# Moving an output weight to the end of a cached-attention kernel, and peeling and halving its last block

## The chip, the cores and the metric

One core of a Trainium2 chip. The metric is the device time of one execution in microseconds (us). The span of a trace is some 2 us shorter than the time of the same execution: the profiled execution of the kernel before took 2552.9 us and its trace spans 2551.1. Where two kernels are compared in time, it is by runs on the same chip; where single steps are compared, it is by the traces.

## The reference, cut to what matters

```python
def _A_ref(x, k_cache, v_cache, wq, wo):          # H = 16 heads, Dh = 256, 65536 keys
    q = (x @ wq).reshape(B, Sq, H, Dh)...          # one query row
    scores = einsum("bhqd,bhkd->bhqk", q, k_cache) * (Dh ** -0.5)
    p = softmax(scores)
    o = einsum("bhqk,bhkd->bhqd", p, v_cache)
    return o.reshape(B, Sq, H * Dh) @ wo           # wo: 4096 x 448

xn = layernorm(x)
s = _A_ref(xn, k_cache, v_cache, wq, wo)
g = silu(silu(xn @ w1) @ w2)
return x + s * g
```

All is bf16. The K and V caches are 537 MB each, and everything else is small.

## The kernel before

The keys are worked through in 64 blocks, four to a head. A block is two K loads and two V loads of 4 MB. VectorE multiplies 19 of every 32 columns of K by the query itself and hands 13 over to ScalarE as products. When a block's scores are there, TensorE and VectorE find one maximum over all partitions ("rows", "gmax", "bcast"), ScalarE takes the exponentials, and TensorE sums them with V ("attend": 64 matmuls of 512 columns) and transposes the result ("turn"). A block's V is loaded and attended while the next block's K is scored.

Two words on TensorE's clock: the profile shows the clock that it was granted as a share of full speed. "Warm" means 1.00, and 32 V matmuls then took 7.07 us; "cold" means 0.50. In a timeline, the bracket at the end of a line gives the time for which the engine had been idle and what ended it.

```python
    def sp_block(i):                                 # the order of the loads
        for t in range(TPB):                         # TPB = 2
            take(sp, kf[t])                          # K buffer t is free
            sp.dma_start(out=Kt[t][:, :], in_=src(Kd, i, t)).then_inc(kl[t], 16)
            take(sp, vf[t])                          # V buffer t is free
            sp.dma_start(out=Vt[t][:, :], in_=src(Vd, i - 1, t)).then_inc(vl[t], 16)
    ...
        need("sp", t8)                               # at the start, once q is computed from W
        sp.dma_start(out=W[:, 0 : NHA * D]..., in_=A_wo...).then_inc(dl["wo"], 16)
    ...
        with nc.Fori(1, NBLK, 1, ...) as i:          # NBLK = 64
            sp_block(i)
            dve_block(i)
            act_block(i)
            act_keep(i - 1)
            pe_bcast()
            pe_attend()
            pe_rows()
            pe_turn()

        last = NBLK - 1                              # V of the last block, and the end
        for t in range(TPB):
            take(sp, vf[t])                          # vf[1] comes with the turn of the block before
            sp.dma_start(out=Vt[t][:, :], in_=src(Vd, last, t)).then_inc(vl[t], 16)
            take(sp, kf[t])
        dve_gmax(); pe_bcast(); act_softmax(last, own)
        ...                                          # the gate g (its reciprocal takes 2.94 us)
        pe_attend(); pe_turn(); act_keep(last)
        ...                                          # weights of 64 blocks, sums, 32 wo matmuls, output
```

## Time and profile before

| | before |
|---|---|
| time, median of 3 runs | 2550.97 us |
| bytes loaded | 1084.3 MB |
| rate of the body | 432 GB/s |
| span of the trace | 2551.1 us |
| last load landed | 2524.9 us |
| TensorE, VectorE, ScalarE busy | 50%, 87%, 57% |

A profile like this is read from the loads inward. The loads fill the body, so only the places where the queue is empty or slow are worth looking at: here the first 64 us and the last 40. The prediction below shows the lines.

### The profile page before, as it was taken

Reading aid. Unit: us, or ns where it says so; the run is one execution under the profiler, and the core shown is the slowest. Engines: PE = TensorE matmul, PEld = TensorE weight load, DVE = VectorE, ACT = ScalarE, POOL = GpSimd, SP = SyncE. Lnnn points to the kernel's source line nnn. Section 1 sums busy time; section 2 is a strip of 40 time slices with the busy share of each in tenths; the row PEclk is TensorE's granted clock in tenths of the full one; section 3 lists DMA queues with packets and bytes.
Section 4 is the critical chain, followed back from the end, with each engine's and each line's share of the span. In section 5 each row is a group of like instructions: output and inputs, shape, how many; then the busy total and the mean of one; then the engine's idle time right before and its main releaser. Section 6 shows DMA issues by size and latency. Waiting matters only on the chain. (4 is left out here: it accounts for less than half of the span.)

```text
span 2551.1 us, 30406 instructions
## 1 busy us (share of the span) xinstructions
PE 1285.1 (50%) x4876; PEld 478.1 (19%) x4876; DVE 2218.4 (87%) x10264; ACT 1445.4 (57%) x6990; POOL 1.2 (0%) x11
## 2 busy tenths in 40 slices
PE   3445545544554554455445445545544554455456
PEld 1111111211211111111112112111111121121122
DVE  5898898888988988988988889889889889898894
ACT  4555565555656555555655556565555555565552
POOL 0000000000000000000000000000000000000000
PEclk7777777777777777777777767777776677677768
DMA  9999999999999999999999999999999999999994
GB/s 386 432 430 434 430 434 430 433 431 432 431 432 432 432 432 431 432 432 432 432 431 432 431 433 431 433 433 432 432 432 431 432 431 432 431 432 432 431 432 210
DMA packets 39535, 1084.43 MB, mean 425 GB/s; under 512 B 4194, under 2 KB 6244, under 8 KB 6308
## 3 DMA queue, kind: packets, MB, share of 16 engines
q1 hardware_dynamic: 39522, 1084.31, 99.0%
q8 instruction: 3, 0.05, 0.0%
q14 instruction: 8, 0.07, 0.0%
q10 hardware_dynamic: 2, 0.00, 0.0%
HBM read 1084.29 MB, written 0.00 MB: 425 GB/s over the span
## 5 line engine op out<-in xcount | busy, mean ns | idle before, releaser
L241 ACT ACTIVATE junk_a<-prod 128x256 bf16<-128x256 bf16 x3328 | 1330.7, 401 | 754.2 <-ACTq L136 754.2
L288 PE MATMUL psO<-V,PV 128*2 128x512 bf16 x4096 | 1170.4, 456 | 1114.0 <-PEq L136 1114.0
L206 DVE CUSTOM_DVE_ANT_0 junk_d<-K,qcur 128x256 bf16<-128x256 bf16 x4864 | 1699.0, 415 | 0.0
L288 PEld LDWEIGHTS psO<-V,PV 128*2 128x2 bf16 x4096 | 388.6, 96 | 1869.4 <-issue 1536.8
L192 DVE TENSOR_TENSOR prod<-K,qcur 128x3328 bf16<-128x3328 bf16 x256 | 483.1, 1887 | 258.7 <-DVEq L136 258.7
L241 ACT ACTIVATION_READ_ACCUMULATOR junk_a<-prod 128x1 f32 x3328 | 619.8, 186 | 0.0
L206 DVE DVE_READ_ACCUMULATOR2_ANT S<- 128x1 f32 x4864 | 380.6, 78 | 0.0
L272 ACT COPY O<-psO 2x512 f32<-2x512 f32 x64 | 36.7, 574 | 222.5 <-ACTq L136 222.5
L309 PE MATMUL ps_t<-eye,O 2*128 2x1 f32 x512 | 68.4, 251 | 50.0 <-PEq L136 50.0
L309 PEld LDWEIGHTS ps_t<-eye,O 2*128 2x128 f32 x512 | 64.9, 191 | 70.5 <-issue 70.5
L274 ACT COPY hist<-ps_t 128x2 f32 x64 | 10.2, 160 | 89.9 <-ACTq L136 89.9
L278 PE MATMUL ps_nb<-gmax,ones_row 1*128 1x1 bf16 x64 | 10.1, 158 | 56.2 <-PEq L136 55.6
L182 DVE COPY qcur<-qb 128x256 bf16 (+1 forms) x64 | 14.6, 227 | 27.4 <-issue 16.1
L261 ACT ACTIVATE PV<-S,hist 128x128 bf16<-128x128 f32 x64 | 25.7, 402 | 2.1
L223 DVE COPY S<-S 128x128 f32<-128x128 f32 x64 | 14.5, 227 | 9.3
L299 PE MATMUL ps_m<-ident,rmax 128*1 128x128 bf16 x64 | 14.1, 220 | 9.3 <-PEq L136 9.3
L171 DVE TENSOR_REDUCE gmax<-ps_m 1x1 bf16<-1x128 f32 x64 | 17.5, 274 | 1.1 <-DVEq L136 1.1
L224 DVE TENSOR_REDUCE rmax<-S 128x1 bf16<-128x128 f32 x64 | 18.0, 281 | 0.0
L278 PEld LDWEIGHTS ps_nb<-gmax,ones_row 1*128 1x128 bf16 x64 | 6.0, 94 | 60.0 <-issue 59.7
L518 DVE TENSOR_REDUCE negM<-hist 128x16 f32<-128x64 f32 x1 | 0.3, 265 | 17.5 <-ACT hist L274 17.5
L441 PE MATMUL ps_a<-xnT,V 128*128 128x1 bf16 (+1 forms) x56 | 6.0, 208 | 15.6 <-DMA V<-in_B_w_dram 15.6
L261 ACT ACTIVATION_READ_ACCUMULATOR PV<-S,hist x64 | 11.9, 186 | 0.0
(56 smaller groups left out, 75.4 us busy)
## 6 DMA issues: line engine op xcount, KB each, us to landing
K<-in_A_k_cache_dram SPq DMA_DIRECT2D x128, 4096.0 KB, 21.5
V<-in_A_v_cache_dram SPq DMA_DIRECT2D x128, 4096.0 KB, 28.7
W<-in_A_wo_dram SPq DMA_DIRECT2D x1, 3584.0 KB, 25.2
W<-in_A_wq_dram SPq DMA_DIRECT2D x1, 3072.0 KB, 10.7
V<-in_B_w_dram SPq DMA_DIRECT2D x1, 1568.0 KB, 38.8
V<-in_B_w_dram SPq DMA_DIRECT2D x1, 1344.0 KB, 34.0
W<-in_A_wq_dram SPq DMA_DIRECT2D x1, 512.0 KB, 13.1
V<-in_B_w_dram SPq DMA_DIRECT2D x1, 224.0 KB, 35.0
```

The costliest lines, as they stand in the source:

```text
L171: dve.reduce_max(out=gmax[0:1, :], in_=ps_m[0:1, :], axis=AX.X).then_inc(gm, 1)
L182: q_t = own(dve.tensor_copy(out=qcur[:, :], in_=qb[:, sub(q0, Dh)]))
L192: m = dve.tensor_tensor(out=prod[k % 2][:, :, :], in0=Kv[:, s * SUB + ND : (s + 1) * SUB, :], in1=qcur[:, None, :].to_broadcast([P, NA, Dh ...
L206: ins = dve.tensor_tensor_reduce(out=junk_d[jk][:, :], in0=Kv[:, s * SUB + j, :], in1=qcur[:, :], scale=1.0, scalar=0.0, op0=ALU.mult, op1 ...
L223: dve.tensor_copy(out=S2[:, :], in_=S[:, :]).then_inc(kf[1], 1)
L224: dve.reduce_max(out=rmax[:, :], in_=S[:, :], axis=AX.X).then_inc(rm, 1)
L241: ins = act.activation(out=junk_a[jk][:, :], in_=prod[k % 2][:, j, :], func=ACT.Identity, accum_out=S[:, a : a + 1],)
L261: act.activation(out=PV[:, :], in_=S2[:, :], func=ACT.Exp, bias=neg, scale=scale, accum_out=hist[:, at(i), 1:2].rearrange("p o s -> p (o s)"),
L272: act.copy(out=O[:, :], in_=psO[:, :]).then_inc(oc, 1)
L278: pe.matmul(ps_nb[:, 0:1], lhsT=ones_row[0:1, :], rhs=gmax[0:1, :], start=True, stop=True).then_inc(bm, 1)
L288: ins = pe.matmul(psO[:, :], lhsT=PV[:, t * KT + 2 * c : t * KT + 2 * c + 2], rhs=Vt[t][:, c * 2 * Dh : (c + 1) * 2 * Dh], start=(t == 0 a ...
L309: ins = pe.matmul(ps_t[:, a : a + 1], lhsT=Ov[:, j, a, :], rhs=eye2[:, j : j + 1], start=(j == 0), stop=(j == 1),)
```

## The change

The intent is to have no load behind which nothing can start, and no work behind the last load that could have been done under it. `wo` is loaded last, in five pieces by heads, into the first K buffer. The last block is taken out of the loop and split in two halves, each with its own maximum and its own entry in the list of partial results, and the second half of its V goes into the weight buffer W, so that it waits for no turn. The weights of the first 15 heads and the gate are worked out under the last attends, and 30 of the 32 wo matmuls need nothing of the last head, so they run while its result is copied, turned and weighted. The core of the diff, with cuts:

```diff
-        need("sp", t8)
-        sp.dma_start(out=W[:, 0 : NHA * D]..., in_=A_wo...).then_inc(dl["wo"], 16)
 ...
         with nc.Fori(
-            1, NBLK, 1,
+            1, NBLK - 1, 1,
 ...
+        take(sp, kf[0]);  K(last, 0) -> Kt[0]
+        take(sp, vf[0]);  V(last - 1, 0) -> Vt[0]
+        take(sp, kf[1]);  halves(Kt[1], src(Kd, last, 1), (kl[1], kh))
+        take(sp, vf[1]);  V(last - 1, 1) -> Vt[1]
+        take(sp, vf[0]);  halves(Vt[0], src(Vd, last, 0), vh[0:2])
+        need("sp", t_wq)
+        halves(W, src(Vd, last, 1), vh[2:4])
+        take(sp, kf[0])
+        for (h0, h1), w in zip(pieces, wl):     # heads 0-4, 4-8, 8-12, 12-14, 14-16
+            sp.dma_start(out=wo_t[:, h0:h1, :], in_=wo_d[:, h0:h1, :]).then_inc(w, 16)
+
+        dve_block(last, halves=True)
+        act_block(last, halves=True)
+        pe_bcast()
+        pe_attend(between=half_max)             # block 62; first half's maximum in between
+        half_max(); dve_gmax(); act_keep(last - 1); pe_turn()
+        act_softmax(last + 1, own, KT, TPB * KT)
+        ... sums, weights and outputs of heads 0 to 14; the gate ...
+        ... 32 V matmuls (first half), 16 V matmuls, turn, 16 V matmuls ...
+        ... 8 wo matmuls, turn, 24 wo matmuls (the last head's weights beside them) ...
```

(Some lines are abridged to what they do; K(i, t) and V(i, t) stand for the load of half t of block i.)

More of the change, by code (lines that the diff above doesn't have):

```diff
@@ L46 @@
     NBLK = H * NB
+    NENT = NBLK + 1
+    H1 = H - 1
+    N1 = H1 * NB
+    NL = NENT - N1
     NA = SUB - ND
@@ L77 @@
     O = pool.tile([2, 2 * Dh], fp32, name="O")
-    hist = pool.tile([P, NBLK, 4], fp32, name="hist")
+    hist = pool.tile([P, NENT, 4], fp32, name="hist")
     ident = pool.tile([P, P], bf16, name="ident")
@@ L95 @@
     negM = pool.tile([P, H], fp32, name="negM")
-    cf = pool.tile([P, H, NB], fp32, name="cf")
-    wgt = pool.tile([P, H, NB], fp32, name="wgt")
+    cf = pool.tile([P, NENT], fp32, name="cf")
+    wgt = pool.tile([P, NENT], fp32, name="wgt")
     tot = pool.tile([P, H], fp32, name="tot")
-    part = pool.tile([P, H, 2, NB], fp32, name="part")
-    OT32 = pool.tile([P, H, 2], fp32, name="OT32")
-    OT = pool.tile([P, NHA], bf16, name="OT")
+    part = pool.tile([P, 2, NENT], fp32, name="part")
+    OT32 = pool.tile([P, 2, H], fp32, name="OT32")
+    OT = pool.tile([P, 2, H], bf16, name="OT")
     tmp = pool.tile([1, D], fp32, name="tmp")
@@ L105 @@
     psO = ps.tile([2, 2 * Dh], fp32, name="psO")
-    ps_m = ps.tile([1, P], fp32, name="ps_m")
+    ps_m = ps.tile([P, P], fp32, name="ps_m")
     ps_nb = ps.tile([P, 1], fp32, name="ps_nb")
@@ L111 @@
     ps_ao = ps.tile([1, D], fp32, name="ps_ao")
-    ps_tot = ps.tile([P, NBLK], fp32, name="ps_tot")
+    ps_tot = ps.tile([P, N1], fp32, name="ps_tot")
     eng = {"pe": pe, "dve": dve, "act": act, "gp": gp, "sp": sp}
@@ L146 @@
     sd, sa = sem("sd"), sem("sa")
-    dl = {n: sem(f"dl_{n}") for n in ("x", "wq", "w12", "wo", "out")}
+    dl = {n: sem(f"dl_{n}") for n in ("x", "wq", "w12", "out")}
+    kh = sem("kh")
+    vh = [sem(f"vh{t}") for t in range(4)]
+    pieces = ((0, 4), (4, 8), (8, 12), (12, 14), (14, 16))
+    wl = [sem(f"wl{t}") for t in range(len(pieces))]
     Kd = A_k_cache[0].rearrange("h (t p c) d -> (h t) p (c d)", p=P, c=KT)
@@ L171, in dve_gmax, with dve_block @@
         dve.reduce_max(out=gmax[0:1, :], in_=ps_m[0:1, :], axis=AX.X).then_inc(gm, 1)
-    def dve_block(i, first=False):
+    def dve_block(i, first=False, halves=False):
         n = [0]
@@ L183, in dve_block, with end @@
         used = [q_t] * 4
+        def end(c0, c1, f):
+            take(dve, pf, 2)
+            take(dve, sd, n[0])
+            n[0], used[:] = 0, [0] * 4
+            dve.tensor_copy(out=S2[:, c0:c1], in_=S[:, c0:c1]).then_inc(f, 1)
+            dve.reduce_max(out=rmax[:, :], in_=S[:, c0:c1], axis=AX.X).then_inc(rm, 1)
         for t in range(TPB):
@@ L189, in dve_block @@
                     take(dve, kl[t], 16)
-                if k >= 2:
+                if halves and k == 3:
+                    take(dve, kh, 16)
+                if k >= 2 and not halves:
                     take(dve, pf)
@@ L200, in dve_block @@
                 m.then_inc(mr, 1)
-                if k == 0 and not first:
+                if (k == 0 and not first) or (k == 2 and halves):
                     dve_gmax()
                 for j in range(ND):
-                    last = t == 0 and s == 1 and j == ND - 1
+                    last = t == 0 and s == 1 and j == ND - 1 and not halves
                     jk = 2 + t if last else j % 2
@@ L215, in dve_block @@
                     )
-                    ins.wait_op(sd, used[jk], "sem-ge")
+                    if used[jk]:
+                        ins.wait_op(sd, used[jk], "sem-ge")
                     if last:
@@ L220, in dve_block, with act_block @@
                         used[jk] = own(ins)
-        take(dve, pf, 2)
-        take(dve, sd, n[0])
-        dve.tensor_copy(out=S2[:, :], in_=S[:, :]).then_inc(kf[1], 1)
-        dve.reduce_max(out=rmax[:, :], in_=S[:, :], axis=AX.X).then_inc(rm, 1)
-    def act_block(i, first=False):
+            if halves:
+                end(t * KT, (t + 1) * KT, kf[t])
+        if not halves:
+            end(0, TPB * KT, kf[1])
+    def act_block(i, first=False, halves=False):
         n = [0]
@@ L254, in act_block, with act_softmax @@
                 act_softmax(i - 1, own)
+            if k == 2 and halves:
+                act_softmax(i, own, 0, KT)
         take(act, sa, n[0])
-    def act_softmax(i, own):
+    def act_softmax(i, own, c0=0, c1=TPB * KT):
         take(act, bm)
@@ L261, in act_softmax @@
         act.activation(
-            out=PV[:, :],
-            in_=S2[:, :],
+            out=PV[:, c0:c1],
+            in_=S2[:, c0:c1],
             func=ACT.Exp,
@@ L268, in act_softmax, with act_keep @@
         ).wait_op(sa, c, "sem-ge").then_inc(pv, 1)
-    def act_keep(i):
+    def act_keep(i, po=psO):
         take(act, od)
-        act.copy(out=O[:, :], in_=psO[:, :]).then_inc(oc, 1)
+        act.copy(out=O[:, :], in_=po[:, :]).then_inc(oc, 1)
         take(act, ho)
@@ L280, in pe_bcast, with pe_keys, pe_attend @@
         ).then_inc(bm, 1)
-    def pe_attend():
+    def pe_keys(po, T, k0, c0, n, start, stop, done=None):
+        for c in range(0, n, 2):
+            ins = pe.matmul(
+                po[:, :],
+                lhsT=PV[:, c0 + c : c0 + c + 2],
+                rhs=T[:, (k0 + c) * Dh : (k0 + c + 2) * Dh],
+                start=(start and c == 0),
+                stop=(stop and c == n - 2),
+            )
+        if done is not None:
+            ins.then_inc(done, 1)
+    def pe_attend(between=None):
         take(pe, pv)
-        n = KT // 2
         for t in range(TPB):
             take(pe, vl[t], 16)
-            for c in range(n):
-                ins = pe.matmul(
-                    psO[:, :],
-                    lhsT=PV[:, t * KT + 2 * c : t * KT + 2 * c + 2],
-                    rhs=Vt[t][:, c * 2 * Dh : (c + 1) * 2 * Dh],
-                    start=(t == 0 and c == 0),
-                    stop=(t == TPB - 1 and c == n - 1),
-                )
-            ins.then_inc(vf[0] if t == 0 else od, 1)
+            pe_keys(psO, Vt[t], 0, t * KT, KT, t == 0, t == TPB - 1, vf[0] if t == 0 else od)
+            if t == 0 and between:
+                between()
     def pe_rows():
@@ L417 @@
         t_q = t9
-        wo_n = W[:, 0 : NHA * D].rearrange("p (n d) -> p n d", d=D)
-        need("sp", t8)
-        sp.dma_start(
-            out=W[:, 0 : NHA * D].rearrange("p (h e) -> p h e", h=H),
-            in_=A_wo.rearrange("(h p a) d -> p h (a d)", p=P, a=2),
-        ).then_inc(dl["wo"], 16)
+        t_wq = t8
         need("dve", t_q0)
@@ L484, with halves @@
         last = NBLK - 1
-        for t in range(TPB):
-            take(sp, vf[t])
-            sp.dma_start(out=Vt[t][:, :], in_=src(Vd, last, t)).then_inc(vl[t], 16)
-            take(sp, kf[t])
-        dve_gmax()
-        pe_bcast()
+        hw = KT * Dh // 2
+        wo_t = Kt[0][:, 0 : NHA * D].rearrange("p (h e) -> p h e", h=H)
+        wo_n = Kt[0][:, 0 : NHA * D].rearrange("p (n d) -> p n d", d=D)
+        wo_d = A_wo.rearrange("(h p a) d -> p h (a d)", p=P, a=2)
+        def halves(T, s, sems):
+            for j in range(2):
+                w = slice(j * hw, (j + 1) * hw)
+                sp.dma_start(out=T[:, w], in_=s[:, w]).then_inc(sems[j], 16)
+        take(sp, kf[0])
+        sp.dma_start(out=Kt[0][:, :], in_=src(Kd, last, 0)).then_inc(kl[0], 16)
+        take(sp, vf[0])
+        sp.dma_start(out=Vt[0][:, :], in_=src(Vd, last - 1, 0)).then_inc(vl[0], 16)
+        take(sp, kf[1])
+        halves(Kt[1], src(Kd, last, 1), (kl[1], kh))
+        take(sp, vf[1])
+        sp.dma_start(out=Vt[1][:, :], in_=src(Vd, last - 1, 1)).then_inc(vl[1], 16)
+        take(sp, vf[0])
+        halves(Vt[0], src(Vd, last, 0), vh[0:2])
+        need("sp", t_wq)
+        halves(W, src(Vd, last, 1), vh[2:4])
+        take(sp, kf[0])
+        for (h0, h1), w in zip(pieces, wl):
+            sp.dma_start(out=wo_t[:, h0:h1, :], in_=wo_d[:, h0:h1, :]).then_inc(w, 16)
+        dve_block(last, halves=True)
+        act_block(last, halves=True)
         n = [0]
@@ L496, in own, with half_max, weights, v @@
             return n[0]
-        act_softmax(last, own)
+        def half_max():
+            pe_rows()
+            pe_bcast()
+        pe_bcast()
+        pe_attend(between=half_max)
+        half_max()
+        dve_gmax()
+        act_keep(last - 1)
+        pe_turn()
+        act_softmax(last + 1, own, KT, TPB * KT)
+        def weights(e0, e1, h0, h1, neg, p_tot):
+            n = e1 - e0
+            b = n // (h1 - h0)
+            def v(T):
+                return T.rearrange("p (h b) -> p h b", b=b)
+            def spread(T):
+                return T[:, h0:h1, None].to_broadcast([P, h1 - h0, b])
+            t = mark("dve", dve.tensor_reduce(
+                out=negM[:, h0:h1], in_=v(neg), axis=AX.X, op=ALU.min
+            ))
+            need("dve", t)
+            t = mark("dve", dve.tensor_tensor(
+                out=v(wgt[:, e0:e1]), in0=spread(negM), in1=v(neg), op=ALU.subtract
+            ))
+            need("act", t)
+            t = mark("act", act.activation(out=wgt[:, e0:e1], in_=wgt[:, e0:e1], func=ACT.Exp))
+            need("dve", t, p_tot[1])
+            t = mark("dve", dve.tensor_tensor(
+                out=cf[:, e0:e1], in0=wgt[:, e0:e1], in1=p_tot[0], op=ALU.mult
+            ))
+            need("dve", t)
+            t = mark("dve", dve.tensor_reduce(
+                out=tot[:, h0:h1], in_=v(cf[:, e0:e1]), axis=AX.X, op=ALU.add
+            ))
+            need("dve", t)
+            t = mark("dve", dve.reciprocal(out=tot[:, h0:h1], in_=tot[:, h0:h1]))
+            need("dve", t)
+            t = mark("dve", dve.tensor_tensor(
+                out=v(cf[:, e0:e1]), in0=v(wgt[:, e0:e1]), in1=spread(tot), op=ALU.mult
+            ))
+            need("dve", t)
@@ new lines, in outputs @@
+        def outputs(e0, e1, h0, h1):
+            b = (e1 - e0) // (h1 - h0)
+            t = mark("dve", dve.tensor_tensor(
+                out=part[:, :, e0:e1],
+                in0=hist[:, e0:e1, 2:4].rearrange("p e a -> p a e"),
+                in1=cf[:, None, e0:e1].to_broadcast([P, 2, e1 - e0]),
+                op=ALU.mult,
+            ))
+            need("dve", t)
+            t = mark("dve", dve.tensor_reduce(
+                out=OT32[:, :, h0:h1],
+                in_=part[:, :, e0:e1].rearrange("p a (h b) -> p a h b", b=b),
+                axis=AX.X,
+                op=ALU.add,
+            ))
+            need("dve", t)
+            return mark("dve", dve.tensor_copy(out=OT[:, :, h0:h1], in_=OT32[:, :, h0:h1]))
@@ L499 @@
+        tt = mark("pe", pe.matmul(
+            ps_tot[:, :], lhsT=ones_sq[:, :], rhs=hist[:, 0:N1, 1], start=True, stop=True
+        ))
+        weights(0, N1, 0, H1, hist[:, 0:N1, 0], (ps_tot[:, :], tt))
+        t_o = outputs(0, N1, 0, H1)
         t = mark("act", act.activation(out=g_e[0:1, :], in_=ps_y, func=ACT.Exp, scale=-1.0))
@@ L509 @@
         ))
-        pe_attend()
+        psO2 = ps_a[0:2, :]
+        take(pe, pv)
+        for j in range(2):
+            pe.wait_ge(vh[j], 16)
+            pe_keys(psO, Vt[0], j * KT // 2, j * KT // 2, KT // 2, j == 0, j == 1,
+                    od if j == 1 else None)
+        take(pe, pv)
+        t15 = mark("pe", pe.matmul(
+            ps_m[:, 0:NL], lhsT=ones_sq[:, :], rhs=hist[:, N1:NENT, 1], start=True, stop=True
+        ))
+        weights(N1, NENT, H1, H, hist[:, N1:NENT, 0], (ps_m[:, 0:NL], t15))
@@ L511 @@
+        act_keep(last)
+        pe.wait_ge(vh[2], 16)
+        pe_keys(psO2, W, 0, KT, KT // 2, True, False)
         pe_turn()
-        t_k = mark("act", act_keep(last))
+        pe.wait_ge(vh[3], 16)
+        pe_keys(psO2, W, KT // 2, KT + KT // 2, KT // 2, False, True, od)
+        t_k = mark("act", act_keep(last + 1, psO2))
         need("dve", t_k)
-        hv = hist[:, :, :].rearrange("p (h b) s -> p h b s", h=H)
-        neg = hv[:, :, :, 0]
-        t = mark("dve", dve.tensor_reduce(out=negM[:, :], in_=neg, axis=AX.X, op=ALU.min))
@@ L519 @@
-        need("dve", t)
-        t = mark("dve", dve.tensor_tensor(
-            out=wgt[:, :, :],
-            in0=negM[:, :, None].to_broadcast([P, H, NB]),
-            in1=neg,
-            op=ALU.subtract,
-        ))
-        need("act", t)
-        t = mark("act", act.activation(out=wgt[:, :, :], in_=wgt[:, :, :], func=ACT.Exp))
-        need("pe", t_k)
-        tt = mark("pe", pe.matmul(
-            ps_tot[:, :], lhsT=ones_sq[:, :], rhs=hist[:, :, 1], start=True, stop=True
-        ))
-        need("dve", t, tt)
@@ L533 @@
-        t = mark("dve", dve.tensor_tensor(
-            out=cf[:, :, :],
-            in0=wgt[:, :, :],
-            in1=ps_tot[:, :].rearrange("p (h b) -> p h b", h=H),
-            op=ALU.mult,
-        ))
-        need("dve", t)
-        t = mark("dve", dve.tensor_reduce(out=tot[:, :], in_=cf[:, :, :], axis=AX.X, op=ALU.add))
-        need("dve", t)
-        t = mark("dve", dve.reciprocal(out=tot[:, :], in_=tot[:, :]))
-        need("dve", t)
-        t = mark("dve", dve.tensor_tensor(
-            out=cf[:, :, :],
-            in0=wgt[:, :, :],
-            in1=tot[:, :, None].to_broadcast([P, H, NB]),
-            op=ALU.mult,
-        ))
@@ L550 @@
-        need("dve", t)
-        for a in range(2):
-            t = mark("dve", dve.tensor_tensor(
-                out=part[:, :, a, :], in0=hv[:, :, :, 2 + a], in1=cf[:, :, :], op=ALU.mult
-            ))
-        need("dve", t)
-        t = mark("dve", dve.tensor_reduce(
-            out=OT32[:, :, :], in_=part[:, :, :, :], axis=AX.X, op=ALU.add
-        ))
-        need("dve", t)
-        t = mark("dve", dve.tensor_copy(
-            out=OT[:, :], in_=OT32[:, :, :].rearrange("p h a -> p (h a)")
-        ))
@@ L565 @@
-        need("pe", t)
-        pe.wait_ge(dl["wo"], 16)
-        for n in range(NHA):
-            ins = pe.matmul(
-                ps_ao[0:1, :],
-                lhsT=OT[:, n : n + 1],
-                rhs=wo_n[:, n, :],
-                start=(n == 0),
-                stop=(n == NHA - 1),
-            )
+        t_l = outputs(N1, NENT, H1, H)
+        need("pe", t_o)
+        for (h0, h1), w in zip(pieces, wl):
+            pe.wait_ge(w, 16)
+            if h0 == pieces[1][0]:
+                pe_turn()
+            for h in range(h0, h1):
+                if h == H1:
+                    need("pe", t_l)
+                for a in range(2):
+                    ins = pe.matmul(
+                        ps_ao[0:1, :],
+                        lhsT=OT[:, a, h : h + 1],
+                        rhs=wo_n[:, 2 * h + a, :],
+                        start=(h == 0 and a == 0),
+                        stop=(h == H1 and a == 1),
+                    )
```

## The prediction

> **What bounds the kernel now.** I read the 40 slices of the page first, then the busy times by stretch, the DMA issues, and last the timeline of the final 60 us. The rows of the slices (DMA share in tenths, then GB/s moved) are
>
> ```profile
> DMA  9999999999999999999999999999999999999994
> GB/s 386 432 430 434 430 434 430 433 431 432 431 432 432 432 432 431 432 432 432 432 431 432 431 433 431 433 433 432 432 432 431 432 431 432 431 432 432 431 432 210
> ```
>
> The transfers fill every slice but the last. So the body can't be shortened by rearranging engines: 1084.3 MB at 432 GB/s are 2510 us. Only the first 64 us and the last 40 us are open. The busy times by stretch (us, busy time and count of each engine, granted clock, DMA share, GB/s) show them:
>
> ```profile
> 32.00:42.00 10.00, 0.00 (x0) 0.00 (x0) 10.00 (x44) 6.69 (x34) 0.00 (x0) 0.50 0.97 350
> 42.00:50.00 8.00, 5.96 (x56) 5.50 (x56) 8.00 (x40) 5.31 (x26) 0.00 (x0) 0.50 1.06 382
> 64.00:2500.00 2436.00, 1225.63 (x4621) 453.93 (x4621) 2162.26 (x10031) 1408.46 (x6839) 0.00 (x0) 0.72 1.00 432
> 2509.00:2512.00 3.00, 2.22 (x13) 0.88 (x10) 1.23 (x7) 0.57 (x1) 0.00 (x0) 1.00 0.05 22
> 2512.00:2525.00 13.00, 8.03 (x42) 3.52 (x42) 3.93 (x3) 1.25 (x5) 0.00 (x0) 1.00 0.80 323
> 2525.00:2551.00 26.00, 18.56 (x74) 7.29 (x74) 3.58 (x12) 0.99 (x3) 0.00 (x0) 0.78 0.00 1
> ```
>
> The queue stands empty from 2509 to 2512, and from 2525 on nothing is loaded while 26 us of closing work run. The timeline of the end (start, length, engine, line, operation) names that work:
>
> ```profile
> 2492.82 19.82 SPq L487 DMA_DIRECT2D V<-in_A_v_cache_dram  x2
> 2502.29 8.70 PE L288 MATMUL psO<-V,PV 128*2 128x512 bf16 x32 [9.57 <-PEq L136]
> 2511.82 1.07 PE L309 MATMUL ps_t<-eye,O 2*128 2x1 f32 x8 [0.78 <-PEq L136]
> 2514.32 7.07 PE L288 MATMUL psO<-V,PV 128*2 128x512 bf16 x32 [1.40 <-PEq L136]
> 2524.96 8.75 PE L288 MATMUL psO<-V,PV 128*2 128x512 bf16 x32 [3.57 <-PEq L136]
> 2535.93 0.27 DVE L518 TENSOR_REDUCE negM<-hist 128x16 f32<-128x64 f32 x1 [17.45 <-ACT hist L274]
> 2538.91 8.30 PE L568 MATMUL ps_ao<-W,OT 128*1 128x448 bf16 x32 [2.47 <-DVE OT L560]
> 2547.24 0.61 DVE L577 TENSOR_TENSOR tmp<-ps_ao,g_f 1x448 f32<-1x448 f32 x1 [8.39 <-PE ps_ao L568]
> 2548.53 0.32 SPq L585 DMA_DIRECT2D out_dram<-out_bf  x1
> ```
>
> The second last V load is issued only when TensorE has turned the block before (2512.3, hence the empty queue). It lands at 2524.9, and then all is serial: 8.75 us of V matmuls, 5.2 us of copies, turn and weights, 8.3 us of wo matmuls, 1.3 us of VectorE, 2.6 us for the output. At the start, wo is loaded where everything behind it waits (start us, length, issue; then the landing time of wo as 25.2 us):
>
> ```profile
> 27.62 0.38 SPq L422 DMA_DIRECT2D W<-in_A_wo_dram  x1
> 41.24 1.70 SPq L165 DMA_DIRECT2D K<-in_A_k_cache_dram  x1
> 62.64 1.89 DVE L192 TENSOR_TENSOR prod<-K,qcur 128x3328 bf16<-128x3328 bf16 x1 [2.85 <-DVEq L136]
> W<-in_A_wo_dram SPq DMA_DIRECT2D x1, 3584.0 KB, 25.2
> ```
>
> wo lands at 52.8. The first MLP weights ahead of it let TensorE start at 43.2, so wo has the queue for 9.6 us (3.67 MB at the 382 GB/s of that stretch), and block 1 starts only at 62.6, when its K has come in behind wo.
>
> **What the Trainium skill says.** "TensorE: Matmul & The Clock Gate", section "The HAM clock gate": the array runs at half clock after an idle window of about 3.4 us and at full clock after about that much activity. The trace agrees: 32 V matmuls took 7.07 us after a pause of 1.40 us, but 8.75 us after one of 3.57 us (clock 0.52 in its first stretch). "DMA: Bandwidth & Descriptors", section "Where 436 GB/s comes from": 435 GB/s at the SBUF ports, but about 358 from HBM per core. The trace has 432, so only the first binds here. "Runtime: NRT & Kernel Launch", section "Instruction fetch mechanics": code is fetched ahead in sequence, and a taken branch may stall. In the trace the loop's turn costs VectorE 16.1 us in 64 starts of a block, 0.25 each; the straight first block shows no hole. So I charge nothing for straight-line code in the peeled block.
>
> **The change part by part.**
> 1. wo leaves the start. K of block 1 is issued at 41.24 anyway (VectorE frees the buffer then), so it streams behind the MLP weights and lands 9.6 us earlier. Against it: queues that are ahead of the slowest run dry before 41.2, up to about 1.5 us. I take 9.3 us of shift for all of the body.
> 2. The last loads. V of block 62, second half, lands at 2502.2 - 9.3 = 2492.9. Behind it come 8.4 MB of V of block 63 without a hole, because the second half goes into W and waits for no turn. At the loop's own rate, 38.9 us for four loads, they take 19.4 us: landed at 2512.3. wo's 3.67 MB in five pieces take again 9.6 us: landed at 2521.9. The hole at 2509 is gone, the bytes are the same.
> 3. VectorE in the peeled block. Its first half ends at 2490.2 - 9.3 = 2480.9. Then come a copy and maximum (0.5), 1.9 + 6.6 us for 13 columns together and 19 single ones, 0.9 for waiting on and taking the first maximum, 8.5 for the last quarter, and 0.5 for the copy and maximum: 2499.8. TensorE asks for it only at 2501.6, so this is hidden by about 2 us.
> 4. TensorE's chain, which I take as the end-setter. Starting at 2492.9: V of block 62 second half, from a cold clock as before, 8.7 (2501.6). Maximum, row, broadcast 1.4 (2503.0). Turn with waits 1.2 (2504.2). Sums of the 15 heads 0.6 (2504.8). V of block 63 first half: 32 at the warm 7.07 (2511.9). Sum of five entries 0.2 (2512.1). 16 V matmuls 3.6 (2515.7; data there at 2507.6). Turn 1.2 (2516.9). 16 more 3.6 (2520.5; data there at 2512.3). wo of four heads, 8 matmuls at the warm 0.187 (20 of them took 3.8 us after 2543), 1.5 (2522.0). Turn 1.1 (2523.1). 24 more wo matmuls 4.5 (2527.6). VectorE 1.3, output 2.6: **2531.5**.
> 5. What disappears from the path: the weights and sums of 15 heads (about 3 us), the silu gate with its 2.94 us reciprocal, most of one cold start, and some of the wo matmuls' cold part. The last head's weights (about 0.7 us of VectorE after the last turn) lie beside the 24 wo matmuls.
> So of some 30 us of idle queue about 19.5 go. The closing matmuls (32 V, 32 V, 32 wo, some 20 us warm) are not removed, and TensorE falls behind the loads.
>
> **The rivals.**
> (a) The loads set the end. The last wo piece lands at 2521.9; four matmuls, VectorE and the output add 4.7: 2527. For it: wo is the last thing loaded. Against it: TensorE can't have begun the last two heads before 2526.9, 5 us later.
> (b) wo at the start was nearly free, because block 1 could not have begun earlier. Then there is no shift: about 2541. Against it is VectorE's wait of 2.85 us before 62.64 on K, and a body that is full to the last.
> (c) The clock falls back to half in the run of small matmuls at 2501 to 2505. Then 16 or so V matmuls cost twice: 3.5 us more, 2535. Before, the same small work between 2511 and 2514 left the clock at 1.00, so I give this one chance in five. The peeled code stalling on fetch, or VectorE's halves overrunning their 2 us, would add 1 to 4 us in the same way.
> (d) Slower than before: loading wo last puts 9.6 us behind the last V, which would cost if nothing left the start and the wo matmuls ran after the last piece alone. That makes about 2550.
>
> **Range and chances.** The sum gives 2531.5, and small unlisted waits push up rather than down: **2532 us**, 0.7% less than before. The low end, 2527, is rival (a); the high end, 2538, holds one lost clock window and a short stall. Faster by 2% would mean 2500 us, under the 2510 us that the bytes alone take: 1%. Slower by 2% has no mechanism of 51 us: 1%. Within 2%: 98%.
>
> **What would show it.** Right: VectorE starts block 1 near 53 to 58 instead of 62.6 (the K is there, its own work ends at 58); full DMA until about 2520, no hole before; TensorE's V and wo matmuls without a pause over 1.5 us from 2493 to 2528, clock 1.00 after 2498; the chain of waits ends in wo matmuls, not in a load. Wrong: wo matmuls that wait for a wo piece (rival a), block 1 at 62 again (rival b), a clock of 0.5 after 2505 (rival c), or VectorE's last maximum later than TensorE's last matmul on block 62.

## The result

| | before | changed |
|---|---|---|
| time, median | 2551.44 us (4 runs) | 2536.03 us (4 runs) |
| range | 2550.57 to 2552.44 | 2534.86 to 2537.42 |
| span of the trace | 2551.1 us | 2533.9 us |

The ratio is 0.994, with a 95% interval of 0.9922 to 0.9957: 0.6% less, the same by the 2% mark. Ratios here are the mean time of one kernel's runs over the mean of the other's of the same rounds, so they are not quite the ratio of the medians.

The page's rows of 40 slices for the changed kernel (DMA share in tenths, GB/s):

```profile
DMA  9999999999999999999999999999999999999998
GB/s 374 434 432 431 432 431 433 432 431 431 432 431 433 432 430 431 432 432 433 432 430 432 431 432 433 431 431 432 431 433 432 431 431 432 431 434 431 431 430 337
```

The last slice now moves 337 GB/s instead of 210. The first moves 374 instead of 386, although a slow load has left it. Busy times by stretch (us, busy time and count of PE, PEld, DVE, ACT, POOL, granted clock, DMA share, GB/s):

```profile
42.00:50.00 8.00, 5.95 (x56) 5.48 (x56) 8.00 (x38) 5.30 (x26) 0.00 (x0) 0.50 0.86 337
80.00:100.00 20.00, 11.04 (x42) 4.33 (x42) 19.52 (x95) 13.36 (x65) 0.00 (x0) 0.76 1.01 433
...
2500.00:2512.00 12.00, 11.38 (x58) 5.08 (x57) 5.07 (x16) 1.86 (x7) 0.00 (x0) 0.99 0.99 419
2512.00:2520.00 8.00, 8.00 (x42) 3.66 (x41) 2.63 (x8) 0.94 (x3) 0.00 (x0) 1.00 1.04 380
2520.00:2524.00 4.00, 4.00 (x21) 1.56 (x19) 0.00 (x0) 0.57 (x1) 0.00 (x0) 1.00 0.46 168
```

The hole at the end is gone: the queue stays full to 2512 and carries wo at 380 GB/s after that. From 42 to 50, where wo used to be, the rate is now 337. The timeline of TensorE at the end (start, length, engine, line, operation):

```profile
2475.20 9.30 PE L307 MATMUL psO<-V,PV 128*2 128x512 bf16 x32 [7.34 <-PEq L140]
...
2495.68 9.30 PE L307 MATMUL psO<-V,PV 128*2 128x512 bf16 x32 [10.10 <-PEq L140]
...
2507.21 7.07 PE L307 MATMUL psO<-V,PV 128*2 128x512 bf16 x32
2514.21 0.39 PE L636 MATMUL ps_m<-hist,ones_sq 128*128 128x5 f32 x2
2514.53 3.62 PE L307 MATMUL ps_a<-W,PV 128*2 128x512 bf16 x16
2518.07 1.10 PE L337 MATMUL ps_t<-eye,O 2*128 2x1 f32 x8
2519.10 3.61 PE L307 MATMUL ps_a<-W,PV 128*2 128x512 bf16 x16
2522.55 1.68 PE L660 MATMUL ps_ao<-K,OT 128*1 128x448 bf16 x8
2524.16 1.10 PE L337 MATMUL ps_t<-eye,O 2*128 2x1 f32 x8
2525.19 4.70 PE L660 MATMUL ps_ao<-K,OT 128*1 128x448 bf16 x24
```

TensorE starts on V of block 62, second half, at 2495.68 (before: 2502.29) and has no pause after that. The chain that ended last is the same list, with two VectorE steps and the output behind it; no load is in it. The wo pieces were issued up to 2514.1 and took at least 10.4 us to land (10.9 is the median of the last two), so the last was there at 2524.5 or shortly after; the first of the four matmuls that use it starts near 2528.9.

### The profile page after: what moved, and what is told of

It is laid out like the page before. It is cut to its first block, busy times and chain, and to the rows that moved or that the text cites. A ratio compares the mean times of both kernels' runs of the same rounds, so it can differ in the third digit from the quotient of the medians.

```text
span 2533.9 us, 30438 instructions
## 1 busy us (share of the span) xinstructions
PE 1283.7 (51%) x4888; PEld 479.5 (19%) x4888; DVE 2219.7 (88%) x10275; ACT 1446.7 (57%) x6996; POOL 1.2 (0%) x11
## 5 line engine op out<-in xcount | busy, mean ns | idle before, releaser
L296 ACT COPY hist<-ps_t 128x2 f32 (+1 forms) x65 | 10.4, 160 | 94.5 <-ACTq L140 94.5
L300 PE MATMUL ps_nb<-gmax,ones_row 1*128 1x1 bf16 x65 | 10.3, 158 | 56.6 <-PEq L140 56.3
L283 ACT ACTIVATE PV<-S,hist 128x128 bf16<-128x128 f32 (+1 forms) x65 | 26.0, 400 | 2.1
L198 DVE COPY S<-S 128x128 f32<-128x128 f32 (+1 forms) x65 | 14.7, 226 | 9.5
L327 PE MATMUL ps_m<-ident,rmax 128*1 128x128 bf16 x65 | 14.3, 220 | 10.3 <-PEq L140 10.3
L199 DVE TENSOR_REDUCE rmax<-S 128x1 bf16<-128x128 f32 (+1 forms) x65 | 18.2, 280 | 0.2 <-issue 0.2
L283 ACT ACTIVATION_READ_ACCUMULATOR PV<-S,hist (+1 forms) x65 | 12.1, 186 | 0.0
## 6 DMA issues: line engine op xcount, KB each, us to landing
W<-in_A_wq_dram SPq DMA_DIRECT2D x1, 3072.0 KB, 11.5
```

Source lines behind the costliest of these rows:

```text
L198: dve.tensor_copy(out=S2[:, c0:c1], in_=S[:, c0:c1]).then_inc(f, 1)
L199: dve.reduce_max(out=rmax[:, :], in_=S[:, c0:c1], axis=AX.X).then_inc(rm, 1)
L283: act.activation(out=PV[:, c0:c1], in_=S2[:, c0:c1], func=ACT.Exp, bias=neg, scale=scale, accum_out=hist[:, at(i), 1:2].rearrange("p o s - ...
L300: pe.matmul(ps_nb[:, 0:1], lhsT=ones_row[0:1, :], rhs=gmax[0:1, :], start=True, stop=True).then_inc(bm, 1)
```

## The experiments

Twelve runs, on three chips, five rounds each. No experiment has a trace of before of its own; its trace is set beside the one shown above. Time differences below are means of the runs. One warning: the comparison with the reference doesn't see an error in the attention sum (a run below leaves matmuls out and still passes it), so that the other variants compute the right thing rests on their code.

### The changed kernel once more

No edit; it is the measure for the three parts that follow.

> The changed kernel once more, for the same chip and rounds as the three parts that follow. The profile of the first run put TensorE's last attend of block 62 at 2495.7 (2502.3 before), so a shift of the body of 6.6 us and not 9.3. My theory for the missing 2.7 us: 1.2 us of chance at the start (block 0's first K was free at 42.4 instead of 41.2) and 1.4 us of an empty queue between 42 and 46. If so, the span wanders with that start by about 1 us and the time is 15 to 18 us under before, ratio 0.993 to 0.994. Rival: the shift is always 6.6, whatever the start.

Measured: 2535.91 us against 2552.92, ratio 0.9935 (0.9921 to 0.9948), 16.8 us less. The five spans are 2532.6 to 2535.9. In its trace the first K of block 0 was scored from 24.97 (25.33 in the first trace of the changed kernel, 24.14 in the trace of before) and block 62's first V half was attended from 2475.52. The start and the shift don't move in step: 0.4 us earlier at the start, 0.3 later at the end.

### wo late, and nothing else

```diff
-        need("sp", t8)
-        sp.dma_start(out=W[...], in_=A_wo...).then_inc(dl["wo"], 16)
 ...
             sp.dma_start(out=Vt[t][:, :], in_=src(Vd, last, t)).then_inc(vl[t], 16)
             take(sp, kf[t])
+        sp.dma_start(out=Kt[0][...], in_=A_wo...).then_inc(dl["wo"], 16)
```

> The kernel before with one thing changed: wo is not loaded at the start but whole, after the last V, into the free first K buffer. My theory: the body moves forward by about 7 us, and wo lands about 9.6 us after the last V (near 2527.5), under the closing work that needs it only near 2532: 7 us faster than before, about 2544. Rival (b), wo at the start was nearly free: no change, 2551. Rival (d), late wo costs what early wo cost: no change or slower, with wo matmuls that wait for the load.

Measured: 2544.95 us, ratio 0.9969 (0.9955 to 0.9982), 7.8 us less than before. TensorE's timeline:

```profile
2494.98 8.84 PE L288 MATMUL psO<-V,PV 128*2 128x512 bf16 x32 [9.42 <-PEq L136]
...
2507.16 7.07 PE L288 MATMUL psO<-V,PV 128*2 128x512 bf16 x32 [1.40 <-PEq L136]
2517.75 8.75 PE L288 MATMUL psO<-V,PV 128*2 128x512 bf16 x32 [3.52 <-PEq L136]
...
2531.70 8.40 PE L567 MATMUL ps_ao<-K,OT 128*1 128x448 bf16 x32 [2.47 <-DVE OT L559]
```

Every line stands 7.2 to 7.3 us ahead of its like in before (2502.29, 2514.32, 2524.96, 2538.91), and the wo matmuls wait for VectorE, as before, not for wo. Moving wo is worth this, and it is under the 9.6 us that wo held the queue. Rivals (b) and (d) fall in their full form.

### wo late, and no hole before the last V

```diff
-            sp.dma_start(out=Vt[1][:, :], in_=src(Vd, last, 1))   # after take(sp, vf[1])
+        need("sp", t_wq)
+        sp.dma_start(out=W[:, :], in_=src(Vd, last, 1)).then_inc(vw, 16)
 ...
-        pe_attend()
+        pe_attend([Vt[0], W], [vl[0], vw])
```

> As the run before, and the second half of the last V goes into the weight buffer without waiting for the turn. My theory: the empty queue of 3 us goes, the last V lands near 2515 and TensorE stays warm across both halves: V matmuls end near 2522, wo matmuls (cold at first, as before) run 2527 to 2535.5, end near 2539.5: 11 to 12 us faster than before, 5 slower than the whole change. Rival: the order of the last loads does not matter because TensorE sets the end: then as the run before, 2544.

Measured: 2541.52 us, ratio 0.9955 (0.9941 to 0.9969), 11.5 us less than before; the span is 2539.7.

```profile
2507.04 7.07 PE L290 MATMUL psO<-V,PV 128*2 128x512 bf16 x32 [1.40 <-PEq L136]
2514.43 7.07 PE L290 MATMUL psO<-W,PV 128*2 128x512 bf16 x32 [0.33 <-PEq L136]
...
2526.70 9.10 PE L571 MATMUL ps_ao<-K,OT 128*1 128x448 bf16 x32 [2.48 <-DVE OT L563]
```

The two attends now follow each other (pause 0.33 us), and the second is warm: 7.07 us instead of 8.75. A first form of this kernel, with the old semaphore for both loads, was refused by the check as a race and went to no chip (there is no entry for it in the record of the runs).

### The loads of before, with the rest of the change

```diff
+        need("sp", t8)
+        sp.dma_start(out=W[...], in_=A_wo...).then_inc(wl[0], 16)
 ...
-        need("sp", t_wq)
-        halves(W, src(Vd, last, 1), vh[2:4])
-        take(sp, kf[0])
-        for (h0, h1), w in zip(pieces, wl): ...
+        take(sp, vf[1])
+        halves(Vt[1], src(Vd, last, 1), vh[2:4])
```

> The changed kernel with the loads of before: wo at the start into the weight buffer, and the last V (two halves) waiting for the turn of block 62. The peeled block, halves with own maxima and hidden closing work stay. My theory: last V lands near 2525.5, 16 V matmuls 3.6, wo and turn 7.3, then 3.9: span near 2540, 10 to 11 us under before. Rival, the gain is all from the loads: little under before, 2548 or more.

Measured: 2544.19 us, ratio 0.9968 (0.9954 to 0.9982), 7.8 us less than before, where 10 to 11 were expected; five spans from 2541.2 to 2545.0. The trace (span 2544.6) shows three terms that I had not counted. The first is that its body stands 1.40 us later than in the trace of before, with the same loads at the start (block 62's first V half is attended at 2484.26 against 2482.86; the traces are from two chips, and why is open). The other two are in these lines:

```profile
2504.73 9.36 PE L307 MATMUL psO<-V,PV 128*2 128x512 bf16 x32 [10.10 <-PEq L140]
...
2516.32 8.69 PE L307 MATMUL psO<-V,PV 128*2 128x512 bf16 x32
```

V of block 62, second half, is attended 20.47 us after the first half (2484.26) and not 19.43 as before; and the attend at 2516.32 runs partly at half clock (8.69 instead of 7.07 us), without a pause ahead of it. These two come back below.

The four runs take the change apart. wo late gives 7.8 us. No hole gives 3.7 more, 11.5. The halves and the hidden closing work give 5.3 more, 16.8. By themselves these last give 7.8, and 11.5 and 7.8 are 19.3, so the two sides of the change overlap by about 2.5 us. (Single runs of one kernel lie up to 4 us apart, so this last difference of four means is the least certain of these numbers.)

### Less work for TensorE at the end

```diff
-        pe_keys(psO2, W, KT // 2, KT + KT // 2, KT // 2, False, True, od)
+        pe_keys(psO2, W, KT // 2, KT + KT // 2, 4, False, True, od)      # 2 of 16 matmuls
```

> The changed kernel with 14 of the last 16 V matmuls left out (a wrong result on purpose); every load and wait stays. If TensorE's chain sets the end, as I hold, the time falls by 14 x 0.22 = 3.1 us (span near 2530.7). If the last loads set it (rival a), it stays as it is. If the wo pieces come in only a little before they are used, it falls by less than 3 us and the trace shows a pause in the wo matmuls.

Measured: 2533.58 us, ratio 0.9927. Three of the five spans are 2530.1, 2530.3 and 2530.5, 3.3 us under the median 2533.8 of the changed kernel (the median of all five is 2530.5); two are 2532.8 and 2533.2. The profile fell on the slowest, and shows why:

```profile
2495.75 9.89 PE L307 MATMUL psO<-V,PV 128*2 128x512 bf16 x32 [9.79 <-PEq L140]
...
2507.86 8.75 PE L307 MATMUL psO<-V,PV 128*2 128x512 bf16 x32
...
2524.50 4.70 PE L660 MATMUL ps_ao<-K,OT 128*1 128x448 bf16 x24
```

Both attends were partly cold. The 24 wo matmuls still took 4.70 us, so they waited for no piece, although they came earlier than in the changed kernel. A slow run of the changed kernel, on another chip (its trace comes below), had the same two cold attends, 9.84 and 8.75 us, so it can be set beside this one: its span is 2536.6, 3.4 us more. Its V came 0.4 us later (2496.14), and the 3.0 us that are left are 14 matmuls at 0.22. TensorE sets the end. Rival (a) falls.

### V first at the start

```diff
         load w1, w2
+        V(0, 0) -> Vt[0];  take(sp, kf[0]);  K(1, 0) -> Kt[0]
     def sp_block(i):
-        K(i, 0)   V(i - 1, 0)   K(i, 1)   V(i - 1, 1)
+        K(i, 1)   V(i - 1, 1)   K(i + 1, 0)   V(i, 0)
```

> The changed kernel with the first V load issued at the start, behind the MLP weights, instead of behind K of block 1 at 42 us; the order of all the others stays. My theory: without wo the queue runs dry from about 42 to 45 because K of block 1 waits for its buffer; with V there the rate between 42 and 46 goes from about 280 to 430 GB/s, which is 1.4 us of data, and the end comes 1.4 us earlier (2534.5 in time, 2532.4 in span). Rival: the low rate there is the end of the MLP weights themselves, and nothing changes.

Measured: 2534.24 us, ratio 0.9933 (0.9919 to 0.9946); the spans are 2530.8 to 2534.7. Beside 0.9935 for the changed kernel this can't be told from nothing. The busy times by stretch say where the gain went:

```profile
42.00:50.00 8.00, 5.95 (x56) 5.47 (x56) 8.00 (x38) 5.31 (x26) 0.00 (x0) 0.50 1.01 432
80.00:100.00 20.00, 12.29 (x48) 5.26 (x46) 19.52 (x86) 11.05 (x53) 0.00 (x0) 0.86 0.97 403
```

The hole at 42 is filled (432 instead of 337 GB/s, 0.76 MB more), and most of it opens again from 80 to 100 (403 instead of 433, 0.6 MB less). By 2475 TensorE is 0.27 us ahead (2474.93 against 2475.20). (Among the traces of the changed kernel and its variants this start lies anywhere from 2474.63 to 2475.68, so 0.27 says little.) My theory was half right: the queue did run dry there, but filling it only moves the lack. The reason stands in VectorE's timeline. The first two lines are from the changed kernel, its first step on block 1 and its first step on the second half of block 2; the third is from this run, its first step on block 1:

```profile
61.01 1.89 DVE L211 TENSOR_TENSOR prod<-K,qcur 128x3328 bf16<-128x3328 bf16 x1
...
114.83 1.89 DVE L211 TENSOR_TENSOR prod<-K,qcur 128x3328 bf16<-128x3328 bf16 x1 [1.91 <-DVEq L140]
63.36 1.89 DVE L218 TENSOR_TENSOR prod<-K,qcur 128x3328 bf16<-128x3328 bf16 x1 [2.82 <-DVEq L140]
```

In the changed kernel VectorE starts every half block from 61 to 113 without waiting for K, so it has no time there to make up for a late start. With V first, K of block 1 comes in behind V: VectorE waits 2.82 us for it and starts 2.35 us later. It frees the K buffers later too (the first K of block 2 is issued at 80.63 instead of 78.27), and the queue runs low from 80 on. In the changed kernel itself VectorE doesn't hold the loads back after 50: from 50 to 160 the queue carries 433 GB/s, and 432 in the kernel before.

### TensorE kept warm, 26 matmuls

```diff
         def half_max_warm():
             half_max()
+            for _ in range(NWARM):     # 26
+                pe.matmul(ps_a[0:2, :], lhsT=ident[:, 0:2], rhs=qb[:, 0:512], start=True, stop=True)
```

> The changed kernel with 26 matmuls of no use on TensorE while it waits for the second V half of block 62 (the pause of 10.1 us before it). My theory: the attend of that half takes 7.1 us warm instead of 8.9 to 9.3, and as TensorE's chain is in series from there, the end moves by the same 1.8 to 2.2 us (2534 in time, 2531.8 in span). Rival: VectorE's maximum or ScalarE's softmax then ends the wait, and less than 1 us comes out.

Measured: 2535.73 us, ratio 0.9939: nothing. The added matmuls were over too soon:

```profile
2485.66 5.77 PE L551 MATMUL ps_a<-qb,ident 128*2 128x512 bf16 x26
2495.81 8.72 PE L308 MATMUL psO<-V,PV 128*2 128x512 bf16 x32 [4.37 <-PEq L141]
```

They ran warm, at 0.22 us each, and left a pause of 4.37 us, so the attend was cold again. The experiment failed by its size and tells nothing of the theory.

### One maximum for the last block

```diff
-        dve_block(last, halves=True); act_block(last, halves=True)
-        pe_attend(between=half_max)
+        dve_block(last, two=True); act_block(last)      # K still loaded in halves
+        pe_attend()
 ...
-        ... 32 V matmuls, od; 16 V matmuls, turn, 16 V matmuls into psO2
+        ... 64 V matmuls into psO, one turn
```

> The changed kernel with one maximum, one softmax and one turn for the last block (K still loaded in halves). My theory: the second half's exponentials come at 2507.7, when TensorE has just become free at 2507.2, so halving wins nothing and costs a turn of 1.0 us: 0.5 to 0.7 us faster than the changed kernel. Rival, that of the change: halves let TensorE start earlier, and it is slower by 1 us or more.

Measured: 2535.43 us, ratio 0.9937, spans 2532.8 to 2535.1: no difference that five rounds can tell. In the trace, from the end of block 62's attend to the end of the span, it takes 28.5 us against 28.9. So the halves' own maxima win nothing, as TensorE is busy with block 62 until the whole maximum is ready; that they lose half a microsecond is what the trace suggests, and the times don't settle it.

### The changed kernel on the third chip

> The changed kernel on this chip, to compare the three that follow: span 2533 to 2535, ratio 0.993 to 0.994.

Measured: 2535.95 us against 2552.50, ratio 0.9935 (0.9921 to 0.9948). The profile fell on its slowest run, with a span of 2536.6; the other spans are 2532.9 to 2534.2. It shows rival (c) at work (first TensorE's timeline, then the busy times by stretch):

```profile
2496.14 9.84 PE L307 MATMUL psO<-V,PV 128*2 128x512 bf16 x32 [9.84 <-PEq L140]
...
2508.20 8.75 PE L307 MATMUL psO<-V,PV 128*2 128x512 bf16 x32
```

```profile
2504.00:2508.00 4.00, 3.38 (x22) 1.97 (x19) 0.71 (x3) 0.58 (x2) 0.00 (x0) 1.00 0.98 418
2508.00:2510.00 2.00, 2.00 (x8) 0.72 (x8) 0.94 (x5) 1.29 (x6) 0.00 (x0) 0.65 1.04 442
2510.00:2512.00 2.00, 2.00 (x6) 0.56 (x5) 1.90 (x5) 0.00 (x0) 0.00 (x0) 0.50 0.90 378
```

The clock fell to 0.50 in the midst of an attend, after a stretch of small matmuls in which TensorE was busy 3.38 of 4 us. That is 1.7 us of the 2.7 by which this span exceeds the first one; 0.5 is the longer cold attend before it, and 0.5 the later V. That the small matmuls are too sparse is not the whole cause: in the first trace the same stretch has the same 3.38 us, and the clock stayed at 1.00. What differs is how late the clock had come back in the attend ahead of them. Of the eleven traces with the peeled block, the three with this fall are, by a narrow margin, those in which that attend took longest (9.36, 9.84 and 9.89 us; 7.07 to 9.30 in the other eight). This is a pattern of the traces that no run tests.

### TensorE kept warm, 44 matmuls

The edit above with `NWARM = 44`.

> The run with matmuls of no use, now 44 of them instead of 26. Those 26 ran warm (5.8 us in all) and ended 4.4 us before V came, so the clock had fallen again and the attend took 8.7 us. My theory: 44 at 0.22 end at about 2495.4, just before V at 2495.7; the attend takes 7.1 us instead of 8.7 to 9.9, and the end comes 1.8 us earlier (span near 2532) and wanders less. Rival: the end is held by something else then, and the span stays above 2533.

Measured: 2533.59 us, ratio 0.9930 (0.9916 to 0.9944), 2.0 us less than the changed kernel; the spans are 2531.3, 2531.3, 2531.4, 2533.5 and 2533.6.

```profile
2485.19 9.66 PE L551 MATMUL ps_a<-qb,ident 128*2 128x512 bf16 x44
2495.34 7.07 PE L308 MATMUL psO<-V,PV 128*2 128x512 bf16 x32 [0.49 <-PEq L141]
```

The attend is warm, and the end follows it: this span is 2.6 us under that of the changed kernel's first trace, of which 2.23 are the shorter attend and 0.34 the earlier V. That is the second sign, after the matmuls left out, that TensorE's chain is in series from here on. What lies behind the two slower runs was not traced.

### The second K half in one transfer

```diff
-        halves(Kt[1], src(Kd, last, 1), (kl[1], kh))
+        sp.dma_start(out=Kt[1][:, :], in_=src(Kd, last, 1)).then_inc(kl[1], 16)
```

> The changed kernel with the second K half of the last block loaded in one transfer instead of two. In six runs with the two transfers the attend of the V behind them starts 20.5 us after the one before, against 19.43 everywhere else; only the run with V loaded first has 19.5. Theory: the two transfers cost that V 1.0 us, so the attend starts 19.4 us after the one before and the end comes 1 us earlier (VectorE's maximum 2 us later, near 2502.6, still before it is asked for). Rival: the delay comes from what is queued around them, and 20.5 us stay.

Measured: 2535.58 us, ratio 0.9936: no change. The attends start at 2475.09 and 2495.47, 20.38 us apart. The theory falls. The late V is not made by the two transfers.

### All that helped or might, together

The edits for V first, one maximum and 44 warming matmuls, and two more: the softmax goes ahead of the second ScalarE copy, and the sums of 15 heads into TensorE's pause.

```diff
-        act_keep(last - 1); pe_turn(); act_softmax(last, own)
+        act_keep(last - 1, mid=lambda: act_softmax(last, own)); pe_turn()
 ...
-        pe_attend()
+        pe_attend(between=fill)        # fill: the ps_tot matmul, then 44 matmuls of no use
```

> V loaded first, one maximum for the last block, softmax before the second copy on ScalarE, the sums of 15 heads moved into TensorE's pause, and 44 matmuls of no use there. If the effects add: V of block 62 at 2494.4, attend warm to 2501.5, row, maximum, broadcast and turn to 2503.5, 14.3 us of V matmuls, 7.2 of wo and turn, 3.9 to the end: span near 2529, 5 us under the changed kernel, ratio near 0.9915. Rival: the last wo piece, which lands near 2523, now binds, or VectorE's maximum comes after the warm attend; then 2530 to 2532.

Measured: 2530.26 us, ratio 0.9913 (0.9900 to 0.9927) to before and 0.9978 to the changed kernel (mean 2530.75 against 2536.41): 5.7 us under it. The spans are 2528.3 to 2530.4. Its profile is of the slowest run, in which V of block 62 came at 2495.90:

```profile
2495.90 7.07 PE L317 MATMUL psO<-V,PV 128*2 128x512 bf16 x32 [1.93 <-PEq L141]
...
2504.80 7.07 PE L317 MATMUL psO<-V,PV 128*2 128x512 bf16 x32
2511.80 0.39 PE L647 MATMUL ps_m<-hist,ones_sq 128*128 128x4 f32 x2
2512.11 7.07 PE L317 MATMUL psO<-W,PV 128*2 128x512 bf16 x32
```

It is the fastest kernel. The warming alone gave 2.0 of the 5.7 us; the rest was not taken apart. The rival of the expectation, that the last wo piece now binds, didn't come true, but only just: the piece was issued at 2514.4 and took at least 10.3 us, so it landed at 2524.7 or later, and the four matmuls that use it start near 2525.4, without a wait. A shorter chain on TensorE would soon meet the loads.

From V's first half to its second it is again 20.50 us, although V is loaded first here too, so the order of the first V is not what made the 19.49 us in that other run.

## Why the prediction was right or wrong

The time came out in the range, 2536.0 against 2532. Point by point, in spans:

**What bounds the kernel.** Right. The body stays at 432 GB/s, and everything was won in the first and last stretch. One reading of the clock was off: the 0.52 quoted for the attend after the pause of 3.57 us belongs to 2526 to 2528; in its first microsecond, up to 2526, the clock was still 1.00.

**Part 1, wo leaves the start: the mechanism right, the size too large.** I took 9.3 us. Measured at the attend of block 62's first V half, the body moved by 7.66 us (2482.86 to 2475.20), and wo late by itself gave 7.8 in time. What was mis-sized is the term "up to about 1.5 us" for queues that run dry, of which I charged only 0.3. K of block 1 is issued at 42.44, when VectorE frees its buffer, and until then nothing but the end of the MLP weights is left to load: from 42 to 50 the queue carried 337 GB/s, 0.76 MB or 1.8 us less than at 432, and 432 with V issued ahead. That is nearly all of the 1.94 us between wo's 9.6 and 7.66. Rival (b) thus had a part of the truth: some 2 us of wo's load lay in a time in which no K buffer was free. My sign for it, block 1 at 53 to 58, also failed: it began at 61.01. But it did so without a wait for K, where before it waited 2.85 us. The rest was VectorE's own work, of which I had left out the MLP steps, and the late first K of block 0. That K is scored from 24.8 to 25.5 in the twelve profiles with wo late, and from 24.1 and 24.5 in the two with wo early. Why is open, as wo is issued only after it, at 27.6.

**Part 2, the last loads.** Right that the hole goes (11.5 against 7.8 us in the two runs that differ by it), and right on wo's rate (380 GB/s). Wrong by 1.05 us on V of block 62, second half: it is attended 20.48 us after the first half in the first trace, where I used the 19.43 of before. Of the eleven traces of the nine kernels with the peeled block, ten show 20.4 to 20.5, also that with the loads of before; only the run with V first shows 19.49, while the three that keep the loop to the end (before, and the two with wo late only) show 19.43. So the delay goes with the peeled block. Neither the two K transfers nor the order of the first V decides it. The nine kernels also load the V behind it in halves, which no run undoes. Its cause stays open.

**Part 3, VectorE hidden.** Right. Its last maximum was ready at 2500.7, and TensorE asked for it at 2504.8.

**Part 4, TensorE's chain sets the end.** Right, and shown twice: 14 matmuls less took 3.0 to 3.3 us off, and a warm attend 2.0. The steps: start 2495.68 instead of 2492.9 (2.8 too early: 1.65 from part 1, 1.05 from part 2, and 0.1 from reading 2502.29 as 2502.2), the cold attend 9.30 instead of 8.7 (0.6), and from its end to the end of the span 28.9 us instead of 29.9, as row, maximum and broadcast took 0.84 us instead of 1.4, and the turns were shorter. Together that is, but for rounding, the 2.4 us between 2531.5 and 2533.9. The rest of the distance to 2536.0 is a slip of scale: I set the span 2551.1 equal to the time 2550.97, but that profiled execution had taken 2552.9. There is some luck in the range: its high end was meant for a lost clock window and a short stall, and 2536.0 used up two thirds of that room although the profiled execution (2536.1) lost no clock window: the room went to the terms just listed.

**Part 5, what disappears.** Right on the gate and the 15 heads, which lie under the V matmuls. That the halves' own maxima help was not my claim, and they don't.

**The rivals.** (a) fell. (b) was part of part 1. (c) is real but not in every execution (three of the eleven traces with the peeled block; I had given it one chance in five): in the traces of the first and second run of the changed kernel the attend after the small matmuls took 7.07 us, in the third 8.75. (d) fell.

## What to carry to other kernels

When loads fill the body, look for the queue's holes at both ends, and ask for each hole what frees the buffer behind it: a load taken out of the start gives back less than it occupied when the load behind it still has to wait for its buffer (7.7 us for 9.6 here). Once the last loads are hidden the engine that uses them last becomes the end, so its chain should be added up matmul by matmul, with cold clock, before more work is moved. A pause of TensorE ahead of such a chain can be filled with matmuls of no use, but only right up to the data.

## What the Trainium skill lacked or had wrong

- "TensorE: Matmul & The Clock Gate", section "What's actually happening", gives an idle window as what brings the half clock back. Here it came back in three traces without a pause ahead of the attend: in the one shown, after a stretch of small matmuls with TensorE busy 3.38 of 4 us, the clock was 0.65 and then 0.50, and 32 matmuls took 8.75 us instead of 7.07. The first trace has the same 3.38 us there and stayed at 1.00. The page has no figure for how little work loses the clock, so the two can't be told apart with it.
- The same page, section "HAM oscillation — how this bites in real kernels", says to leave no idle gap over about 3.4 us and lacks what filling one is worth: 26 matmuls that ended 4.37 us before the data gave nothing (8.72 us for the attend), 44 that ended 0.49 us before it gave 7.07 us and 2.0 us of time.
- "DMA: Bandwidth & Descriptors", section "Specifications", gives 512 B as the least transfer for line rate. The wo load, in rows of 1792 B, ran at 380 to 382 GB/s at either end of the kernel (with the last MLP weights beside it at the start), the long rows of K and V at 432. That the length of the rows is the reason was not tested.
- No page that I read explains why the V of the peeled block is attended 1.0 us later (20.4 to 20.5 us between two attends instead of 19.43).
